# A fused attention and feed-forward kernel on one core: its list of pieces in another order

## The chip, the cores and the metric

The kernel runs on one core of one Trainium2 chip. The metric is the device time of one execution in microseconds (us), the median of the runs shown. The engines are named as in the profile: PE (TensorE, the matmuls), PEld (its weight loads), DVE (VectorE), ACT (ScalarE), POOL (GpSimd) and SP (SyncE, which issues most DMAs).

## The reference

The input x has 2048 rows of 512 numbers. The output is x plus an attention branch plus a feed-forward branch, both of the normalized x:

```python
xn = _layernorm(x, axis=-1)
return x + _A_ref(xn, A_wq, A_wk, A_wv, A_wo, A_beta) + _B_ref(xn, B_w1, B_w2)
```

The feed-forward branch is silu(xn w1) w2 with 1792 hidden columns. The attention branch has 32 heads of 16 columns and works on four segments of 512 rows. In each segment a causal softmax attention is mixed, by a gate for each head, with a linear attention that reads a memory M, z built from all segments before:

```python
for s in range(N):
    logits = jnp.einsum('bhqd,bhkd->bhqk', qs, ks) * scale + mask
    a_dot = jnp.einsum('bhqk,bhkd->bhqd', _softmax(logits), vs)
    num = jnp.einsum('bhld,bhde->bhle', phi(qs), M)
    den = jnp.einsum('bhld,bhd->bhl', phi(qs), z)[..., None] + 1e-06
    outs.append(g * num / den + (1.0 - g) * a_dot)
    M = M + jnp.einsum('bhld,bhle->bhde', phi(ks), vs)
    z = z + jnp.einsum('bhld->bhd', phi(ks))
```

Then the segments are put together and multiplied by wo.

## The kernel before

The whole kernel is cut into 1349 small pieces, and one string, ORDER, names them in the order in which their instructions are recorded. Nothing is scheduled later: each engine does its own instructions in that order, and waits on semaphores only for what its instructions need. So ORDER sets, for each engine, what stands behind what.

A word of ORDER is a piece and its numbers: the segment s first, then a tile or a part. The words that the prediction speaks of:

- `xc xd xs xq xi xg` take the sums and roots of the layer norm of a 128-row tile t, `Nv` normalizes it on DVE, `X` turns it on PE (with `Xa`, `Xv` the copies to xnT), `XD` turns it by a transposing DMA from SP instead.
- `k q v` are the products of a segment with wk, wq and wv, in parts; `kv qv vv` copy them from PSUM on DVE, `ka qa va` on ACT; `kp` and `kf` split k by odd and even heads.
- `h` is a product with w1, `ha` its tanh on ACT, `hv` the rest of the silu on DVE.
- `S0` to `S71` are the batches of scores: the matmuls into psS (line 724), the exponential from psS to a buffer Pb on ACT (line 730), and the causal selects on POOL (line 744). psS fills four PSUM banks and has one buffer, so the scores of a batch wait for the exponential of the one before.
- `E` and `O` weigh v with Pb, for even and odd heads (line 791). `Ev Ea` and `Ov` copy the sums out of PSUM and move the rows of the softmax denominators by two small DMAs each (`move_sums`); `Om` merges odd into even on DVE.
- `fp fa fv` and `gp ga gv` make phi of k and of q on POOL, ACT and DVE; `t` turns phi(k) by a transposing DMA (L441); `m` is the product for M (psM), `mv mw` add and mask it.
- `s sv r w` make the denominators and their reciprocals, `R` and `W` the same for the last segment; `z` and `d` spread them by DMAs (`spr`), `zv` and `dv` multiply, `n` is the product with M and `nv` adds it to oT.
- `o`, `oc`, `od` and `oh` are products with w2 and wo into psO, of whole, half and quarter width and of the last tile's halves. `xl` loads a tile of x again, `st` adds it and stores the output, `sh` does so for the last two halves.
- `lw` loads w2 and wo from ACT's queue, `busy` keeps PE at work while the first inputs come.

All PSUM tiles but psS share a pool of four banks, which go round in the order of ORDER: a product that takes a bank waits until the result that was there has been copied out. Products are done as one 128x128 matmul, or, between the `E`, `O` and `m` words, as four matmuls of 32 columns (`narrow`), so that the tiling of PE changes seldom.

Of the kernel before, what the change touches and what calls it, by code (L numbers as in the profile page):

```python
# [25 lines left out]
S6 fa0.3 k1.2.0 k1.2.1 k1.2.2 h0.5.0 h0.5.1 h0.5.2 q1.1.0 h0.5.3 ha0.5 k1.2.3 kv1.2 q1.1.1 q1.1.2 hv0.5
S8 h0.7.0 q1.1.3 qv1.1 h0.6.0 h0.6.1 h0.6.2 h0.6.3 ha0.6 fv0.3 E1 Ev1 k1.0.0
S9 hv0.6 h0.7.1 h0.7.2 h0.7.3 Om0 ha0.7 k1.0.1 k1.0.2 kp1.2 q1.0.0 q1.0.1 q1.0.2 fp0.1 Nv9 XD9 xs12 k1.0.3 kv1.0 kp1.0
S10 h0.8.0 hv0.7 h0.8.1 h0.8.2 h0.8.3 ha0.8 h0.9.0 h0.9.1 q1.0.3 t0.3 Nv10 XD10 h0.9.2 h0.9.3 qv1.0
S13 hv0.8 O1 Ov1 xs15 v1.0.0 v1.0.1 v1.0.2 ha0.9 v1.0.3 vv1.0 h0.10.0 h0.10.1 bmask  # L30
S12 k1.1.0 k1.1.1 k1.1.2 t0.2 k1.1.3 kv1.1 h0.10.2 h0.10.3 ha0.10 hv0.9 h1.0.0 Om1 h1.0.1 h1.0.2
# [6 lines left out]
S24 h1.8.0 h1.8.1 h1.8.2 h1.8.3 m0.0 mv0.0 q2.3.0 q2.3.1 qv2.3 ha1.8 hv1.8
S18 v2.1.0 v2.1.1 vv2.1 ga1.0 k2.0.0 o0.2.7 oc0.2.5.0 ha1.11 sv0 r0.1 o0.2.4 k2.0.1 kv2.0 xg12.4
S22 fv1.3 v2.2.0 v2.2.1 vv2.2 o0.2.1 ga1.1 gp1.2 o0.2.6 o0.0.3 o0.0.13 od0.2.11.1 hv1.11 r0.2 o0.0.10  # L40
S20 o0.2.0 oc0.0.2.0 r0.3 lw1 o0.2.2 od0.0.0.2 oc0.2.10.1 h1.1.0 h1.1.1 h1.1.2 h1.1.3 kp2.1 E4 r0.0 od0.0.0.1 ha1.1 gate w0 gv1.1 kp2.0 z0.1
S28 o0.0.6 hv1.1 z0.2 o0.0.8 z0.3 o0.0.11 o0.0.5 Ev4 oc0.0.7.1 Om3 z0.0 o0.2.8 o0.0.12 ga1.2 O4 Ov4
S26 q2.0.0 q2.0.1 h1.7.0 h1.7.1 h1.7.2 h1.7.3 gv1.2 ha1.7 qv2.0 oc0.2.10.0 od0.0.0.3 oc0.0.2.1
S23 fp1.2 od0.2.11.3 h1.4.0 hv1.7 h1.4.1 h1.4.2 Nv14 o0.2.12 h1.4.3 ha1.4 od0.2.11.0 oc0.0.7.0 zv0.3 h1.9.0 o0.2.13 h1.9.1
S25 h1.9.2 h1.9.3 ha1.9 Nv12 XD12 o0.2.3 oc0.2.5.1 gp1.0 zv0.2 o0.2.16 o0.0.16 hv1.4 zv0.0 XD14 zv0.1 E5 o0.0.17 Ev5 hv1.9
S29 fa1.2 o0.2.17 o0.2.14 k2.3.0 gv1.0 k2.3.1 kv2.3 h1.2.0 h1.2.1 h1.2.2
S27 o0.0.9 mw0.0 O5 o0.2.15 Ov5 o0.2.9 Nv13 fp1.0 XD13 h1.2.3 ha1.2 od0.2.11.2 fv1.2 st0.2 t1.2 o0.0.14 o0.0.15
S31 o0.0.4 h1.13.0 h1.13.1 h1.13.2 h1.13.3 ha1.13 o0.3.8 Om5 o0.3.11 o0.3.16 hv1.2 o0.3.9
S30 o0.3.14 h1.12.0 h1.12.1 h1.12.2 h1.12.3 t1.3 Nv15 hv1.13 ha1.12 XD15 od0.0.0.0 o0.1.16 od0.1.8.2 o0.1.17 o0.1.12 hv1.12 oc0.1.9.0
S33 o0.0.1 od0.1.8.3 o0.3.1 xl0.1 od0.1.8.0 st0.0 oc0.1.3.0 o0.1.13 oc0.1.3.1 xl0.3 gp1.3 Om4 fa1.0 o0.1.2 E6 o0.1.0  # L50
S32 kp2.3 Ev6 O6 Ov6 o0.3.17 o0.3.13 o0.3.10 o0.1.6 oc0.3.2.1 o0.1.15 m1.2 fa2.0 mv1.2 fv1.0
S35 o0.1.4 q2.2.0 q2.2.1 qv2.2 fp2.0 ga1.3 v2.0.0 v2.0.1
S34 h1.5.0 h1.5.1 o0.1.14 o0.1.11 t1.0 vv2.0 h1.5.2 oc0.3.0.1 xl1.0 gv1.3 fp1.1 h1.5.3 ha1.5 E7
# [8 lines left out]
S44 dv1.2 q3.0.0 q3.0.1 Ev9 mw1.0 oc1.2.3.1 oc1.2.11.1 od1.2.1.3 fv2.2 gp2.2 n1.2 d1.3 O8 nv1.2 fa2.3 Ov8 xl1.2 oc1.2.3.0
S45 oc1.2.11.0 o1.2.9 h2.7.0 h2.7.1 ha2.7 qv3.0 fv2.3 v3.2.0 v3.2.1 vv3.2
S48 hv2.7 h2.6.0 h2.6.1 ha2.6 k3.2.0 k3.2.1 z1.3 dv1.3 o1.0.4 dv1.0 kv3.2 ga2.2 o1.0.0 oc1.0.7.1
S47 od1.0.1.3 hv2.6 h2.0.0 od1.2.1.2 h2.0.1 ha2.0 dv1.1 zv1.3 t2.2 n1.3 Om8 o1.0.6 o1.2.5 o1.0.16 nv1.3 hv2.0 gp2.1 o1.0.13
# [877 lines left out]
```

## Time and profile before

| | us |
|---|---|
| median of the runs | 220.22 |
| lowest and highest of three | 219.97, 221.33 |
| span of the profiled execution | 218.2 |
| PE busy | 210.9 |
| PEld busy | 116.1 |
| DVE busy | 181.3 |
| ACT busy | 184.1 |
| POOL busy | 127.4 |

The span goes from the first to the last instruction of the program in the profiled execution; the profile gives no other time for that execution, and the runs' times are those of whole executions. In a row of a timeline the columns are start, duration, engine, line, operation and tiles; behind them in brackets stands the idle time before and what ended it. In a row of waits stand the engine, what it waited for, and the total, the number and the longest. In a row for a line of code the three numbers after the count are the shortest, median and longest duration in ns. In a row by stretches stand the stretch and its length, then the busy time and instruction count of PE, PEld, DVE, ACT and POOL, the granted clock, the DMA share and GB/s.

### The profile page before, as it was taken

How to read it: one execution, taken by the hardware profiler on the slowest of the kernel's cores; microseconds unless marked ns; L12 is line 12 of the kernel's file. 1: busy time of each engine (PE TensorE's matmuls, PEld its weight loads, DVE VectorE, ACT ScalarE, POOL GpSimd, SP SyncE). 2: the span in 40 equal slices, each digit the busy share in tenths (PEclk: the TensorE clock that was granted, in tenths of full speed). 3: DMA queues.
4: the chain of work that ended last, by engine and by line, in shares of the span. 5: the costliest groups of instructions: out<-in, count | busy, mean ns of one | idle time of the engine just before them, and what ended most of it. 6: DMA issues, size and time to landing. Idle time of an engine off the chain costs nothing.

```text
span 218.2 us, 9267 instructions
## 1 busy us (share of the span) xinstructions
PE 210.9 (97%) x3982; PEld 116.1 (53%) x4006; DVE 181.3 (83%) x370; ACT 184.1 (84%) x173; POOL 127.4 (58%) x203
## 2 busy tenths in 40 slices
...
ACT  3799999999999999999999999999989998942000
...
PEclk9999999999999999999999999999999999999999
...
DMA packets 33273, 19.60 MB, mean 90 GB/s; under 512 B 14672, under 2 KB 33232, under 8 KB 33232
## 3 DMA queue, kind: packets, MB, share of 16 engines
...
## 4 chain that ended last, share of the span: by engine, by line
PE 92%; DMA 3%; ACT 2%; issue 1%; SPq 1%; DVE 0%
PE ps L336 26%; PE psO L338 17%; PE ps L338 16%; PE psS L724 11%; PE psO L336 9%; PE psV L791 8%; PE psS L338 4%; DMA wk_sb<-in_A_wk_dram 3%; ACT Pb L730 2%; PE psM L452 1%; SPq L169 0%; SPq L158 0%; PE ps L509 0%; ACT th L492 0%; DVE o_half L668 0%
## 5 line engine op out<-in xcount | busy, mean ns | idle before, releaser
L730 ACT ACTIVATE Pb<-psS 128x2048 bf16<-128x2048 f32 x72 | 135.2, 1878 | 4.7 <-PE psS L724 2.4
L744 POOL TENSOR_SCALAR_AFFINE_SELECT Pb<-Pb 128x512 bf16<-128x512 bf16 (+2 forms) x88 | 62.3, 718 | 22.4 <-ACT Pb L730 19.6
L497 DVE SCALAR_TENSOR_TENSOR hT<-th,ps 128x512 bf16<-128x512 bf16 x56 | 38.0, 682 | 10.1 <-ACT th L492 9.4
L744 POOL TENSOR_SCALAR_AFFINE_SELECT lows<-Pb 64x512 bf16<-64x512 bf16 (+1 forms) x40 | 24.3, 607 | 32.0 <-ACT Pb L730 24.9
L338 PE MATMUL psO<-w_sb,hT 128*32 128x512 bf16 (+2 forms) x696 | 41.4, 321 | 0.0
L336 PE MATMUL ps<-xnT,w_sb 128*128 128x512 bf16 (+1 forms) x177 | 35.9, 330 | 0.2 <-issue 0.2
L492 ACT ACTIVATE th<-ps 128x512 bf16<-128x512 f32 x56 | 33.0, 594 | 3.5 <-PE ps L338 3.1
L338 PEld LDWEIGHTS <-hT 128*32 128x32 bf16 x864 | 21.5, 96 | 14.6 <-issue 3.1
L338 PE MATMUL ps<-xnT,w_sb 128*32 128x512 bf16 (+1 forms) x408 | 24.8, 349 | 0.0
L724 PE MATMUL psS<-qT,k 32*128 32x64 bf16 (+3 forms) x512 | 23.0, 233 | 0.2
L336 PEld LDWEIGHTS <-w_sb 128*128 128x128 bf16 x178 | 16.4, 98 | 11.9 <-issue 1.2
L336 PE MATMUL psO<-w_sb,hT 128*128 128x512 bf16 (+2 forms) x82 | 20.5, 324 | 0.7 <-issue 0.6
L791 PEld LDWEIGHTS <-Vz 128*32 128x32 bf16 x768 | 16.1, 97 | 9.5 <-issue 0.6
L791 PE MATMUL psV<-Pb,Vz 128*32 128x448 bf16 (+7 forms) x512 | 21.0, 286 | 0.0
L724 PEld LDWEIGHTS <-k 32*128 32x128 bf16 x512 | 9.3, 92 | 21.2 <-issue 20.4
L336 PE MATMUL ps<-xnT,wk_sb 128*128 128x256 bf16 (+1 forms) x63 | 14.4, 326 | 0.4 <-DMA wk_sb<-in_A_wk_dram 0.2
L724 PE MATMUL psS<-qT,kT 16*128 16x448 bf16 (+3 forms) x256 | 14.7, 269 | 0.0
L338 PEld LDWEIGHTS <-w_sb 128*32 128x32 bf16 x408 | 10.3, 96 | 6.7 <-issue 1.7
L621 DVE SCALAR_TENSOR_TENSOR o_out<-psO,x_res 128x512 bf16<-128x512 f32 x14 | 9.4, 679 | 5.0 <-PE psO L338 3.9
L336 PEld LDWEIGHTS <-hT 128*128 128x128 bf16 x92 | 8.5, 98 | 9.6 <-issue 2.1
L828 DVE CAST odd<-psV 128x512 bf16<-128x512 f32 x16 | 11.0, 687 | 2.4 <-PE psV L791 2.4
L338 PE MATMUL psO<-wo_sb,oT 128*32 128x512 bf16 x140 | 12.8, 379 | 0.0
...
## 6 DMA issues: line engine op xcount, KB each, us to landing
...
```

The source lines that it names most:

```text
L336: return [nc.tensor.matmul(out, lhsT=lhsT, rhs=rhs, start=start, stop=stop, skip_group_check=True)]
L338: nc.tensor.matmul(out[c : c + 32], lhsT=lhsT[:, c : c + 32], rhs=rhs, start=start, stop=stop, tile_position=(0, c), skip_group_check=True,)
L452: nc.tensor.matmul(psM[32 * g : 32 * g + 32, i, :].rearrange("p (r d) -> p r d", d=DH), lhsT=st["phiK", dt][:, j, 32 * g : 32 * g + 32], r ...
L492: nc.scalar.activation(out=th[:], in_=sts[s]["h", ft][:, :], func=AF.Tanh, scale=0.5)
L497: nc.vector.scalar_tensor_tensor(out=st["hT"][:, ft, :], in0=st.pop(("th", ft))[:], scalar=1.0, in1=st.pop(("h", ft))[:, :], op0=ALU.add, ...
L621: out = nc.vector.scalar_tensor_tensor(out=o_out[:], in0=st.pop(("psO", j)), scalar=0.5, in1=st["x", j][:], op0=ALU.mult, op1=ALU.add)
L724: nc.tensor.matmul(psS[:, g, c : c + q2 - q1], lhsT=keys[rows], rhs=st["qT"][rows, dt, q1:q2], start=True, stop=True, tile_position=(32 * ...
L730: exp = nc.scalar.activation(out=blocks(Pb, b).rearrange("p y g c -> p g y c"), in_=psS[:, :, :].rearrange("p g (y c) -> p g y c", c=BLOCK ...
L744: over[id(Pb)].append(nc.gpsimd.affine_select(out=out, in_=in_, compare_op=ALU.is_ge, fill=0.0, base=base, pattern=[[0, out.shape[1]], [1, ...
L791: nc.tensor.matmul(psV[32 * g : 32 * g + 32, q0 : q0 + nq].rearrange("p (y c) -> p y c", y=weights.shape[2]), lhsT=Vzs[s % 2][:, kt, 4 * d ...
L828: copy(out=odd[:], in_=sts[s].pop(("psV", 1))[:, :])
```

## The change

ORDER is the same 1349 words in another order. No function, buffer, load or instruction's form changes, but some products pass between the one wide and the four narrow matmuls, since that follows from the words around them: PE has 4003 matmuls in place of 4006. The sequence of the batches `S` is the same. The diff, cut to lines that the prediction speaks of:

```diff
-S3 h0.3.0 h0.3.1 q0.3.1 q0.3.2 h0.3.2 tanh XD5 h0.3.3 k0.3.0 Nv7 XD7 q0.3.3 qv0.3 k0.3.1 xs8 ha0.3
-S4 Nv4 h0.1.0 k0.3.2 h0.1.1 hv0.3 XD4 h0.2.0 h0.2.1 h0.2.2 h0.2.3 ha0.2 xs9 k0.3.3 kv0.3 hv0.2
...
-S17 h1.10.3 k1.3.0 hv1.0 k1.3.1 k1.3.2 k1.3.3 kv1.3 fp1.3 h0.12.0 h0.12.1 xs14 m0.2 mv0.2 ha1.10 h0.12.2
-S21 fv0.1 q1.3.0 q1.3.1 q1.3.2 q1.3.3 qv1.3 h1.3.0 hv1.10 gp1.1 h0.12.3 ha0.12 t0.1 h1.3.1 h1.3.2 t0.0 h1.3.3
-S14 hv0.12 k2.2.0 h0.11.0 h0.11.1 k2.2.1 h0.11.2 h0.11.3 xl0.0 h0.13.0 ha1.3
...
-S42 kv3.0 o1.2.6 o1.2.2 o1.2.10 d1.1 h2.11.0 h2.11.1 ha2.11 o1.2.0 t2.0 vv3.0 zv1.1 gv2.3 o1.2.4 fp2.2 zv1.2
-S39 hv2.11 q3.2.0 ga2.1 q3.2.1 qv3.2 d1.0 v3.3.0 v3.3.1 va3.3 E9
...
+S3 q0.3.1 hv0.0 h0.3.0 h0.3.1 fp0.0 h0.3.2 q0.3.2 q0.3.3 k0.3.0 h0.3.3 Nv5 qv0.3 ha0.3
+S4 k0.3.1 h0.1.0 h0.2.0 h0.1.1 XD6 XD5 XD4 tanh h0.2.1 Nv7 h0.2.2 hv0.3 h0.2.3 ha0.2 h0.1.2 k0.3.2 fp0.2
...
+S17 h1.10.3 Ov2 hv1.0 k1.3.0 k1.3.1 k1.3.2 k1.3.3 h0.12.0 ha1.10 m0.2 h0.12.1 kv1.3
+S21 h0.12.2 h0.12.3 Om0 q1.3.0 kp1.1 q1.3.1 q1.3.2 mv0.2 h1.3.0 hv1.10 bmask fv0.1 q1.3.3 ha0.12 h1.3.1 h1.3.2
+S14 h0.11.0 qv1.3 h0.11.1 k2.2.0 k2.2.1 h1.3.3 xs14 h0.11.2 hv0.12 gp1.1 mw0.2 ha1.3 h0.11.3 t0.0
...
+S42 o1.2.2 o1.2.0 o1.2.6 gv2.3 h2.11.0 od1.2.1.1 vv3.0 ga2.1 z1.1 fv2.2 h2.11.1 ha2.11 zv1.2 xl1.2 o1.2.10 dv1.2 o1.2.4 kv3.0
+S39 q3.2.0 v3.3.0 v3.3.1 va3.3 z1.3 od1.2.1.3 hv2.11 fp2.3 q3.2.1 E9
...
```

At the start the words from the turn of x tile 2 on are `X2.1 Xa1.1 k0.1.0 tb Nv3 X3.1 Xv2.1 k0.1.1` before and `X2.1 xi3 Nv3 Xa1.1 tb X3.1 Xv2.1 k0.0.0` now. In the last line, of S71, the stretch that the prediction adds up reads now:

```
od2.3.10.3 o3.2.0 o3.2.15 o3.0.16 oh13.1 od3.1.0.0 n3.0 o3.2.10 o3.1.4 od3.0.3.1 oc3.1.10.1 st2.3 Om15 xl3.0 o3.1.16 o3.0.10 oh9.0 nv3.0 zv3.3 oh14.1
```

Two places show how the instructions move. The first is SP's queue between the copies of the sums of O0 and the product m0.2. The rows into zraw are the small moves of `move_sums`, those into xnT transposes of x tiles (`XD`), those into phiK the two turns of phi(k) that m0.2 needs (`t0.3` and `t0.2`), and x_res is `xl0.2`. Before:

```order
L813 DMA zraw_102<-odd_740 4x256 x2
L813 DMA zraw_102<-oraw_869 4x256 x2
L857 DMA_TRANSPOSE xnT_139<-xn_t_911 128x4x128
L441 DMA_TRANSPOSE phiK_960<-pk_850 128x4x128
L857 DMA_TRANSPOSE xnT_139<-xn_t_962 128x4x128
L813 DMA zraw_102<-odd_1024 4x256 x2
L441 DMA_TRANSPOSE phiK_1085<-pk_635 128x4x128
L614 DMA x_res_1139<-in_A_x_dram 128x512
L857 DMA_TRANSPOSE xnT_139<-xn_t_1147 128x4x128
```

And now, from the same moves of O0 on:

```order
L813 DMA zraw_102<-odd_759 4x256 x2
L441 DMA_TRANSPOSE phiK_786<-pk_642 128x4x128
L813 DMA zraw_102<-oraw_884 4x256 x2
L857 DMA_TRANSPOSE xnT_139<-xn_t_926 128x4x128
L614 DMA x_res_1044<-in_A_x_dram 128x512
L813 DMA zraw_102<-odd_1050 4x256 x2
L857 DMA_TRANSPOSE xnT_139<-xn_t_946 128x4x128
L441 DMA_TRANSPOSE phiK_1090<-pk_844 128x4x128
L857 DMA_TRANSPOSE xnT_139<-xn_t_944 128x4x128
```

One turn of phi(k) (t0.2) has moved ahead of the transposes of x; the other (t0.3) has moved behind the load x_res, the next moves of odd sums and a second transpose of x. The load x_res takes the buffer that the transpose just ahead of it reads.

The second place is DVE's queue in the last 15 us of the program. The rows L608 are `nv3.1`, `nv3.0` and `nv3.3`, L589 are `zv`, L835 is `Om15`, and the first L621 is `st2.3`. Before:

```order
L608 TENSOR_TENSOR oT_5227<-ps_5283,oT_5227 128x512
L589 TENSOR_TENSOR oT_5227<-spr_5202,oraw_4205 128x512
L835 COPY_PREDICATED oraw_5018<-omask_130,odd_5022 128x256
L608 TENSOR_TENSOR oT_5227<-ps_5344,oT_5227 128x512
L589 TENSOR_TENSOR oT_5227<-spr_5307,oraw_5018 128x512
L608 TENSOR_TENSOR oT_5227<-ps_5403,oT_5227 128x512
L621 SCALAR_TENSOR_TENSOR o_out_5451<-psO_4858,x_res_5354 128x512
```

And now:

```order
L608 TENSOR_TENSOR oT_5318<-ps_5348,oT_5318 128x512
L621 SCALAR_TENSOR_TENSOR o_out_5435<-psO_4846,x_res_5190 128x512
L835 COPY_PREDICATED oraw_5001<-omask_130,odd_5020 128x256
L608 TENSOR_TENSOR oT_5318<-ps_5414,oT_5318 128x512
L589 TENSOR_TENSOR oT_5318<-spr_5363,oraw_5001 128x512
L608 TENSOR_TENSOR oT_5318<-ps_5459,oT_5318 128x512
```

The store of the last tile of segment 2 has moved from behind the last two additions to oT to a place ahead of both.

More of the change, by code (lines that the diff above doesn't have):

```diff
@@ L26 @@
[L26 to L31, printed above, removed]
@@ L38 @@
[L38 to L42, printed above, removed]
@@ L43 @@
[L43 to L53, printed above, removed]
@@ L60 @@
-S42 kv3.0 o1.2.6 o1.2.2 o1.2.10 d1.1 h2.11.0 h2.11.1 ha2.11 o1.2.0 t2.0 vv3.0 zv1.1 gv2.3 o1.2.4 fp2.2 zv1.2
-S39 hv2.11 q3.2.0 ga2.1 q3.2.1 qv3.2 d1.0 v3.3.0 v3.3.1 va3.3 E9
[L62 to L65, printed above, removed]
@@ new lines @@
+S13 hv0.8 kp1.0 ha0.9 h0.10.0 h0.10.1 xs15 O1 XD8 v1.0.0 xl0.2 v1.0.1 Ov1 XD11 v1.0.2 v1.0.3
+S12 h0.10.2 vv1.0 h0.10.3 h1.0.0 hv0.9 xs13 h1.0.1 k1.1.0 t0.3 k1.1.1 XD10 k1.1.2 h1.0.2 ha0.10 XD9 k1.1.3 kv1.1
+S15 hv0.10 h1.0.3 E2 ha1.0 h1.10.0 h1.10.1 Om1 Ev2 h1.10.2 O2
+S17 h1.10.3 Ov2 hv1.0 k1.3.0 k1.3.1 k1.3.2 k1.3.3 h0.12.0 ha1.10 m0.2 h0.12.1 kv1.3
+S21 h0.12.2 h0.12.3 Om0 q1.3.0 kp1.1 q1.3.1 q1.3.2 mv0.2 h1.3.0 hv1.10 bmask fv0.1 q1.3.3 ha0.12 h1.3.1 h1.3.2
+S14 h0.11.0 qv1.3 h0.11.1 k2.2.0 k2.2.1 h1.3.3 xs14 h0.11.2 hv0.12 gp1.1 mw0.2 ha1.3 h0.11.3 t0.0
```

103 lines of the change are left out of this document (63 added, 40 removed).

## The prediction

> **What bounds the kernel now.** First the page: busy shares, slices, and the chain that ended last.
>
> ```profile
> span 218.2 us, 9267 instructions
> PE 210.9 (97%) x3982; PEld 116.1 (53%) x4006; DVE 181.3 (83%) x370; ACT 184.1 (84%) x173; POOL 127.4 (58%) x203
> ACT  3799999999999999999999999999989998942000
> PEclk9999999999999999999999999999999999999999
> PE 92%; DMA 3%; ACT 2%; issue 1%; SPq 1%; DVE 0%
> ```
>
> TensorE is busy in 97% of the span at full clock and holds 92% of the chain. ScalarE is as full until about 190 us and then has nothing to do. Busy time can hide small waits, since one matmul's record overlaps the next, so I read the busy time by stretches, then PE's own waits.
>
> ```profile
> 12.00:190.00 178.00, 175.54 (x3263) 92.32 (x3286) 154.89 (x311) 172.78 (x153) 121.86 (x185) 1.00 0.32 80
> 0.00:12.00 12.00, 10.09 (x102) 8.37 (x105) 8.75 (x26) 6.87 (x16) 4.24 (x16) 1.00 0.84 274
> PE psS L864 <- DVE zraw L188: 1.1, 1, 1.1
> PE psO L336 <- issue: 1.0, 6, 0.2
> PE ptr L845 <- DVE xn_t L315: 0.5, 1, 0.5
> PE ps L336 <- DMA wk_sb<-in_A_wk_dram: 0.2, 1, 0.2
> ```
>
> From 12 to 190 us PE is idle for 178.00 - 175.54 = 2.46 us, and its list of waits names no engine there that costs more than 0.2 us. The named waits lie in the first 9 us. So the next question is what one round, from one batch of scores (line 724) to the next, is made of. The timeline of PE and of ACT over two rounds:
>
> ```profile
> 104.88 0.21 PE L724 MATMUL psS<-qT,k 32*128 32x64 bf16 x4
> 107.26 0.21 PE L724 MATMUL psS<-qT,k 32*128 32x64 bf16 x4
> 107.60 1.90 PE L336 MATMUL ps<-xnT,w_sb 128*128 128x512 bf16 x8
> 109.34 0.38 PE L336 MATMUL psO<-w_sb,hT 128*128 128x512 bf16 x1
> 109.65 0.40 PE L724 MATMUL psS<-qT,k 32*128 32x64 bf16 x8
> 105.33 1.88 ACT L730 ACTIVATE Pb<-psS 128x2048 bf16<-128x2048 f32 x1
> 107.10 0.58 ACT L376 CAST kT<-ps 128x512 bf16<-128x512 f32 x1
> 107.72 1.88 ACT L730 ACTIVATE Pb<-psS 128x2048 bf16<-128x2048 f32 x1
> 109.49 0.59 ACT L492 ACTIVATE th<-ps 128x512 bf16<-128x512 f32 x1
> ```
>
> A round takes 107.26 - 104.88 = 2.38 us. Eight products take 109.34 - 107.60 = 1.74 us, 0.217 each. Two loops close at the same length: PE's (the scores and nine products) and that of scores and exponential, for psS has one buffer: the exponential that starts at 105.33 ends at 107.21, the next scores start at 107.26. A round with one small ScalarE instruction beside the exponential cannot be shorter than 2.38. First and last batch:
>
> ```profile
> L724 PE MATMUL psS<-qT,k x512: 184/198/348, 12.0 to 190.1; 32*128 32x64 bf16 x104, 32*128 32x192 bf16 x24, 32*128 32x448 bf16 x22, 32*128 32x320 bf16 x21
> ```
>
> 71 rounds take 178.1 us. By columns, the matmuls between them are 740.75 products of 512: 740.75 x 0.217 = 160.7, which leaves 17.4 / 71 = 0.245 us a round for entering and leaving the row-tiled scores. There is hardly anything in this stretch to be won by order; there is something to be lost.
>
> **The change part by part.** It removes no work. Both lists have the same 1349 words, the batches of scores in the same sequence, and 144 changes of PE's tiling. Some products pass from the four narrow matmuls to one wide one or back, for no time:
>
> ```profile
> 107.67 1.83 PE ps L336 x8
> 117.36 1.84 PE ps L338 x32
> ```
>
> Eight wide matmuls take 1.83, 32 narrow ones 1.84. Up to the last batch the new list has 741.25 products, half a product more, and half a product fewer behind it: zero.
>
> *The start.* The transposes of x tile 3 (X3) now stand ahead of the first product of k.
>
> ```profile
> 6.59 0.40 PE L845 MATMUL ptr<-ident,xn_t 128*128 128x128 bf16 x4 [0.52 <-DVE xn_t L315]
> 8.54 0.39 PE L336 MATMUL ps<-xnT,wk_sb 128*128 128x256 bf16 x2 [0.24 <-DMA wk_sb<-in_A_wk_dram]
> 8.77 0.39 PE L845 MATMUL ptr<-ident,xn_t 128*128 128x128 bf16 x4
> PEld L724 <- ACT qT L399: 0.3, 1, 0.3
> ```
>
> X3 can fill the 0.24 us in which PE waits for wk. But the first scores wait for ScalarE's copy of q in any case, and that comes behind the same two copies. Between 0 and -0.24; taken: 0, since the wait for qT (0.3) swallows it.
>
> *Short rounds.* Only a round with less than 2.38 us of PE work costs anything. S3 has one product less and S4 one more than before, which is an exchange. S17 loses a quarter of h0.12 to the next round; before, S17's round is
>
> ```profile
> 48.55 0.40 PE L724 MATMUL psS<-qT,k 32*128 32x192 bf16 x8
> 50.98 0.40 PE L724 MATMUL psS<-qT,k 32*128 32x192 bf16 x8
> ```
>
> 50.98 - 48.55 = 2.43; less 0.217 is 2.21, so PE waits 2.38 - 2.21 = 0.17 us for the exponential. Term: +0.17. Behind it the queue of PE alone waits.
>
> *Rounds with two small ScalarE instructions.* One such instruction moves from S18 to S22, from S39 to S42, from S48 to S47 and from S56 to S50. A round with two needs on ACT 1.77 + 0.6 + 0.6 = 2.97 (starts 105.33, 107.10, 107.72), and together with the next round 2.97 + 2.38 = 5.35 between the first scores and the last. PE's work over the two, at 0.217 a product and 0.245 a round: S22 with S20 22.75 products, 5.43; S42 with S39, S47 with S46 and S50 with S52 22 products each, 5.26. The old S39 with S44 had 21.75, 5.21, and PE's list of waits has none there. Between 0 and 0.09 for each of three; taken: 0.05 in all.
>
> *VectorE, whose results give PE's banks back.* psS takes four PSUM banks, the other four go round; a late copy stops PE. In the new list many VectorE words stand nearer to the PE word that needs them (33 of 170 edges within 0.25 us of PE's work, before 12 of 171). But the engine runs when its inputs are there, not at its place in the list. Adding up its queue with the rows' durations ahead of each such edge, 33 of PE's waits (those of the scores left out) had under 0.25 us to spare before and 36 have it now: no net loss, but new thin places, at O15 (behind the store st2.1), k2.2.0, k2.1.0 and q2.1.0. Before, such margins cost nothing. Bounds: 0, and at O15 a whole store; taken 0.2.
>
> *The end.* VectorE's store st2.3 now stands ahead of nv3.0. Rows of before:
>
> ```profile
> 206.79 0.69 DVE L608 TENSOR_TENSOR oT<-ps,oT 128x512 bf16<-128x512 f32 x1 [0.72 <-PE ps L338]
> 205.62 0.45 DVE L835 COPY_PREDICATED oraw<-omask,odd 128x256 int32<-128x256 int32 x1
> 209.46 0.69 DVE L621 SCALAR_TENSOR_TENSOR o_out<-psO,x_res 128x512 bf16<-128x512 f32 x1 [0.45 <-PE psO L338]
> 215.31 0.42 DVE L668 SCALAR_TENSOR_TENSOR o_half<-psS,x_res 128x256 bf16<-128x256 f32 x1 [0.18 <-PE psS L338]
> ```
>
> From od2.3.10.3 to oh14.1, which needs nv3.0, PE has 10 products, 2.17 us; VectorE needs 0.16 (a matmul's 0.38 less its 0.217) + 0.69 + 0.45 + 0.69 = 1.99. It fits. The last instructions stay PE's last half-product, the 0.42 us o_half and its store. Term: 0.
>
> Sum: 218.2 + 0.17 + 0.05 + 0.2 = 218.6 us of span. The three runs of before have a median of 220.22, 2.0 over the profiled span (219.97 to 221.33): 220.6.
>
> **The rivals.** *Slower by VectorE behind GpSimd.* What VectorE does on SBUF alone is uneven, what reads PSUM is not:
>
> ```profile
> L835 DVE COPY_PREDICATED oraw<-omask,odd x16: 384/468/1143, 37.7 to 205.6; 128x256 int32<-128x256 int32 x16
> L589 DVE TENSOR_TENSOR oT<-spr,oraw x16: 408/422/839, 77.6 to 207.4; 128x512 bf16<-128x512 bf16 x16
> L497 DVE SCALAR_TENSOR_TENSOR hT<-th,ps x56: 672/680/690, 20.2 to 199.4; 128x512 bf16<-128x512 bf16 x56
> ```
>
> A stretched copy takes 1.143 - 0.384 = 0.76 us more. If one falls just ahead of each of three thin edges (a predicated copy, Om13, does stand ahead of st2.1 and O15), PE loses 3 x 0.7 = 2.1: 222.7. Against it: the medians (0.468 and 0.422) lie near the minimum, so most such copies are not held up, and of the thin edges of before none was hit. It decides from three hits on. The Trainium skill, "SBUF — State Buffer", section Who interferes with whom, says that VectorE and GpSimd share a port pair as an exclusive lock: the one that starts second waits out the other's whole instruction. These rows agree (uneven on SBUF alone, even from PSUM). By that rule a hit costs up to one GpSimd select; with the median of the row below, three cost 2.0, and the sum would be 222.6 in place of 222.7.
>
> ```profile
> L744 POOL TENSOR_SCALAR_AFFINE_SELECT Pb<-Pb x88: 409/657/1096, 14.9 to 192.7; 128x512 bf16<-128x512 bf16 x32, 128x256 bf16<-128x256 bf16 x32, 128x1024 bf16<-128x1024 bf16 x24
> ```
>
> *Slower by a late transposing DMA.* SP's order changes: t0.3, the last turn of pk that m0.2 needs, now comes behind xl0.2, which waits until XD8 has landed, Ov1's two moves and XD11. Adding up SP's queue, it is issued some 3.6 us ahead of m0.2; with a landing of 2.4 (an estimate, twice the issue of the row below) 1.2 us are left, before over 3. The upper bound is the one landing that the chain shows:
>
> ```profile
> L441 SPq DMA_TRANSPOSE phiK<-pk x12: 1191/1216/1275, 39.7 to 139.7; - x12
> 2.68 5.81 DMA wk_sb<-in_A_wk_dram
> ```
>
> At 5.81 PE would stand 5.81 - 2.4 - 1.2 = 2.2 us: 222.8. Against it: the engines are lightly used there, unlike at 2.68.
>
> *Faster.* If the new order took away all 2.46 us that PE idles between 12 and 190, it would be 217.8. Nothing in the list does, as every round is held by two loops.
>
> **How the numbers follow.** No change to speak of, 220.6, own range 219.7 to 222.0: 0.78. GpSimd rival 0.11, late DMA 0.07, faster 0.02, other stalls of over 2 us 0.02. A measurement of this kernel tells about 1% (2.2 us) from no change; so faster 0.02, within 1% 0.78, slower 0.20. The range goes from 219.5 (no stall, the start's 0.24 won, the lowest run's 1.8 beside the span: 219.7, and 0.2 for the runs' own spread) to 223.0, past both rivals.
>
> **What would show it.** Right: PE busy near 175.5 between 12 and 190, first and last scores again near 12.0 and 190.3, no PE wait for DVE or DMA over 0.3 us, S17 to S21 at 2.38, nv3.0 done before oh14.1. Wrong: a later last batch of scores with waits of PE for DVE at O15, k2.2.0, k2.1.0 or q2.1.0, or at psM for phiK; or a first batch well before 11.9.

## The result

The changed kernel takes 222.97 us, the median of six runs (221.47 to 224.20); the kernel before took 220.38 beside it (219.87 to 221.33). The ratio is 1.0122, with a 95% interval of 1.0088 to 1.0155: slower by 2.6 us where no change was forecast. Here and below the ratios leave out two runs of the kernel before, of 736.97 us (beside e0 to e3) and 223.50 us (beside e4 to e7), which lie over 1.5% above its fastest. The list of waits of the changed kernel's TensorE (what waited, for what, total, times, longest) and its chain by engine:

```profile
span 221.5 us, 9262 instructions
PE 64%; ACT 9%; DVE 8%; DMA 6%; POOL 5%; issue 3%; SPq 2%; DVEq 0%; POOLq 0%; ACTq 0%
PE psS L864 <- DVE zraw L188: 1.1, 1, 1.1
PE ps L338 <- DVE hT L497: 1.0, 1, 1.0
PE ptr L845 <- DVE xn_t L315: 0.8, 1, 0.8
PE psV L791 <- POOL Pb L744: 0.8, 1, 0.8
```

The span is 3.2 us longer than before's (3.3 by the rounded figures). The chain says that it is no longer one engine's: PE had 92% of it and has 64%, the rest lies with ACT, DVE, DMA and POOL. The second and fourth rows of the waits are new; the first and third lie ahead of the first scores.

Where the time went can be read without any guess, since both lists have the same 72 batches of scores in the same order. The first matmul of line 724 of each batch, from the timelines of PE, gives this difference to before in us (left: its start in the kernel before; the other columns are the experiments below). Each column is one execution; that of e2 and of e3 is the slowest run of its kernel, that of e9 the fastest. So the columns say where time is lost, and the medians say how much.

```
batch before  after     e0     e1     e2     e3     e5     e6     e8    e11     e7     e9    e10
S0     11.95  +0.15  +0.27  +0.22  +0.32  -0.05  +0.13  +0.40  +0.59  +0.23  +0.18  -0.22  +0.12
S4     21.55  +0.11  +0.24  +0.19  +0.28  +0.75  +0.10  +0.36  +0.56  +0.20  +0.17  -0.23  +0.11
S7     23.93  +0.15  +0.28  +0.22  +0.32  +1.34  +0.13  +0.40  +0.59  +0.23  +0.18  -0.22  +0.12
S17    48.55  +0.58  +0.71  +0.63  +1.04  +1.93  +0.65  +0.82  +1.07  +0.84  +0.18  -0.20  +0.15
S21    50.98  +0.53  +0.66  +0.58  +0.99  +1.87  +0.60  +0.76  +1.01  +0.79  +0.18  -0.20  +0.14
S28    71.21  +0.53  +0.66  +0.59  +0.99  +1.87  +0.60  +0.77  +1.02  +0.79  +0.18  -0.20  +0.15
S26    73.62  +0.64  +0.77  +0.70  +1.10  +1.99  +0.71  +0.88  +1.13  +0.90  +1.07  -0.20  +0.15
S25    78.45  +0.63  +0.76  +0.69  +1.10  +1.98  +0.70  +0.87  +1.13  +0.89  +1.06  -0.20  +0.14
S29    80.84  +1.58  +1.73  +0.69  +2.07  +1.98  +0.70  +0.87  +1.13  +0.89  +1.16  -0.20  +0.14
S61   147.29  +1.68  +1.83  +0.79  +2.17  +2.08  +0.80  +0.97  +1.22  +0.99  +1.18  -0.03  +0.17
S54   150.00  +1.35  +2.38  +0.46  +2.62  +2.65  +1.51  +0.65  +0.90  +0.66  +1.17  -0.03  +1.04
S62   167.03  +1.31  +2.34  +0.42  +2.58  +2.62  +1.47  +0.61  +0.85  +0.62  +1.17  -0.03  +0.95
S63   169.59  +2.83  +3.86  +1.94  +2.79  +2.83  +1.69  +0.82  +1.07  +0.84  +1.17  +2.22  +0.94
S67   171.99  +2.89  +3.92  +2.00  +3.29  +3.33  +1.75  +0.88  +1.13  +0.89  +1.17  +2.22  +0.95
S65   179.34  +2.93  +3.96  +2.04  +3.33  +3.37  +1.79  +0.92  +1.17  +0.94  +1.76  +2.21  +0.94
S66   181.89  +3.10  +4.13  +2.21  +4.46  +3.97  +3.62  +1.34  +1.34  +1.11  +1.76  +2.22  +0.95
S71   189.99  +2.99  +4.02  +2.10  +4.35  +3.86  +3.51  +1.23  +1.23  +1.00  +1.76  +2.21  +0.94
end   218.24  +3.22  +4.13  +2.04  +4.30  +3.79  +3.46  +1.18  +1.17  +0.95  +1.77  +2.23  +0.97
```

In the column "after" two steps carry the loss: S25 to S29 (0.95) and S62 to S63 (1.52). A step also holds the work that was moved from one round to another, 0.217 us for each product. Counting the matmuls between the batches in both traces takes this out: S61 to S54 (-0.33) has one and a half products fewer and loses nothing, and S62 to S63 has one product more and loses 1.30. Rounds with the same work that take longer are S8 to S9 (0.15) and S15 to S17 (0.25); S17 to S21 has one product less and gains only 0.05, so it loses 0.17. With the start (0.15) that makes 2.97 in all; the table has 2.99 at S71.

**S25 to S29.** The timeline of POOL from the select of S22 to that of S23 (start, duration, tiles, in brackets the idle time before and what ended it), in the kernel before, with the products of E5 on PE that read the last of them, and then in the changed one:

```profile
67.11 0.51 POOL L297 TENSOR_SCALAR rstd_all<-mv_all 128x4 f32<-128x4 f32 x1
67.70 1.02 POOL L300 TENSOR_TENSOR rstd_all<-rstd_all,expo 128x4 f32<-128x4 f32 x1
68.79 0.66 POOL L744 TENSOR_SCALAR_AFFINE_SELECT lows<-Pb 64x512 bf16<-64x512 bf16 x1
79.26 0.63 POOL L744 TENSOR_SCALAR_AFFINE_SELECT Pb<-Pb 128x512 bf16<-128x512 bf16 x1
79.97 0.72 PE L791 MATMUL psV<-Pb,Vz 128*32 128x512 bf16 x16
```

```profile
68.83 0.65 POOL L744 TENSOR_SCALAR_AFFINE_SELECT lows<-Pb 64x512 bf16<-64x512 bf16 x1 [1.28 <-ACT Pb L730]
69.55 1.09 POOL L744 TENSOR_SCALAR_AFFINE_SELECT Pb<-Pb 128x1024 bf16<-128x1024 bf16 x1
70.73 0.71 POOL L297 TENSOR_SCALAR rstd_all<-mv_all 128x4 f32<-128x4 f32 x1
71.53 1.02 POOL L300 TENSOR_TENSOR rstd_all<-rstd_all,expo 128x4 f32<-128x4 f32 x1
76.96 0.86 POOL L385 TENSOR_SCALAR k<-kT,pm_odd 128x512 bf16<-128x512 bf16 x1
77.79 0.71 POOL L385 TENSOR_SCALAR k<-kT,pm_even 128x256 bf16<-128x256 bf16 x1
80.53 1.76 POOL L744 TENSOR_SCALAR_AFFINE_SELECT Pb<-Pb 128x512 bf16<-128x512 bf16 x2
81.55 0.72 PE L791 MATMUL psV<-Pb,Vz 128*32 128x512 bf16 x14 [0.77 <-POOL Pb L744]
```

L297 and L300 are the word `xg12.4`, the roots for x tiles 12 to 15. Before, they filled POOL's idle time ahead of S22's select. Now POOL idles there for 1.28 us, and the two instructions (0.71 and 1.02) stand behind that select; from there on the queue has hardly a gap until S23's select (the first of the two at 80.53), for which E5 waits 0.77 us. Before, this select ended at 79.26 + 0.63 = 79.89, and E5's products that read it started at 79.97: an edge with 0.08 us to spare.

**S62 to S63.** SP's issues of the spreads in the changed kernel (two for each), and from its chain the transfer:

```profile
159.30 4.17 SPq L577 DMA_DIRECT2D spr<-rz  x6
164.02 1.27 SPq L577 DMA_DIRECT2D spr<-rz  x2
```

```profile
164.69 3.89 DMA spr<-rz
168.60 0.03 DVE phiQT L599
```

Then DVE's timeline and PE's:

```profile
166.68 0.42 DVE L599 TENSOR_TENSOR phiQT<-spr,phiQT 128x512 bf16<-128x512 bf16 x1
168.60 0.63 DVE L599 TENSOR_TENSOR phiQT<-spr,phiQT 128x512 bf16<-128x512 bf16 x1 [1.50 <-DMA spr<-rz]
169.15 1.30 DVE L589 TENSOR_TENSOR oT<-spr,oraw 128x512 bf16<-128x512 bf16 x1
170.38 1.27 DVE L497 SCALAR_TENSOR_TENSOR hT<-th,ps 128x512 bf16<-128x512 bf16 x2
171.11 0.40 PE L338 MATMUL ps<-phiQT,Mbf 128*32 128x512 bf16 x4 [0.95 <-DVE hT L497]
```

The first six are `d2.2`, `z2.0` and `d2.0`, the last two `d2.3`, which lands 3.9 us after the issue of its second half began. `dv2.3` (168.60) stops DVE for 1.50 us, `zv2.0` behind it takes 1.30 instead of 0.42, and only then come `hv3.1` and `hv3.12`. The first of these empties the bank that `n2.0` needs, and PE stands for 0.95. `dv2.3` is itself stretched, 0.63 for 0.42.

### The profile page after: what moved, and what is told of

Read it like the earlier page. It is cut to its first block, busy times and chain, and to the rows that moved or that the text cites. A ratio compares the mean times of both kernels' runs of the same rounds, so it can differ in the third digit from the quotient of the medians.

```text
span 221.5 us, 9262 instructions
## 1 busy us (share of the span) xinstructions
PE 212.2 (96%) x3979; PEld 115.5 (52%) x4003; DVE 180.9 (82%) x370; ACT 184.2 (83%) x173; POOL 126.3 (57%) x203
## 4 chain that ended last, share of the span: by engine, by line
PE 64%; ACT 9%; DVE 8%; DMA 6%; POOL 5%; issue 3%; SPq 2%; DVEq 0%; POOLq 0%; ACTq 0%
PE ps L336 18%; PE ps L338 11%; PE psO L338 10%; PE psS L724 8%; PE psO L336 7%; PE psV L791 7%; ACT Pb L730 7%; DMA spr<-rz 5%; POOL Pb L744 3%; SPq L577 2%; POOL k L385 1%; PE psS L338 1%; DMA x_lo<-in_A_x_dram 1%; DVE stats L286 1%; POOL lows L744 1%
## 5 line engine op out<-in xcount | busy, mean ns | idle before, releaser
L744 POOL TENSOR_SCALAR_AFFINE_SELECT lows<-Pb 64x512 bf16<-64x512 bf16 (+1 forms) x40 | 23.1, 578 | 36.8 <-ACT Pb L730 35.2
L338 PE MATMUL psO<-w_sb,hT 128*32 128x512 bf16 (+2 forms) x700 | 42.0, 322 | 0.0
L336 PE MATMUL ps<-xnT,w_sb 128*128 128x256 bf16 (+1 forms) x178 | 38.6, 328 | 0.5 <-issue 0.2
L338 PE MATMUL ps<-xnT,w_sb 128*32 128x512 bf16 (+1 forms) x376 | 24.2, 353 | 0.0
L336 PEld LDWEIGHTS <-w_sb 128*128 128x128 bf16 x186 | 17.0, 98 | 13.6 <-issue 2.5
L336 PE MATMUL psO<-w_sb,hT 128*128 128x512 bf16 (+2 forms) x85 | 21.6, 325 | 0.1
L385 POOL TENSOR_SCALAR k<-kT,pm_odd 128x512 bf16<-128x512 bf16 x15 | 10.6, 706 | 9.4 <-ACT kT L376 8.4
L336 PE MATMUL ps<-xnT,wk_sb 128*128 128x512 bf16 (+1 forms) x62 | 14.2, 328 | 0.3 <-issue 0.2
L338 PEld LDWEIGHTS <-w_sb 128*32 128x32 bf16 x376 | 9.2, 96 | 7.0 <-issue 1.9
```

The lines of the kernel that those rows point to most:

```text
L336: return [nc.tensor.matmul(out, lhsT=lhsT, rhs=rhs, start=start, stop=stop, skip_group_check=True)]
L338: nc.tensor.matmul(out[c : c + 32], lhsT=lhsT[:, c : c + 32], rhs=rhs, start=start, stop=stop, tile_position=(0, c), skip_group_check=True,)
L385: nc.gpsimd.tensor_scalar(out=to, in0=frm, scalar1=keep[:, 0:1], scalar2=1.0, op0=ALU.mult, op1=ALU.mult)
L744: over[id(Pb)].append(nc.gpsimd.affine_select(out=out, in_=in_, compare_op=ALU.is_ge, fill=0.0, base=base, pattern=[[0, out.shape[1]], [1, ...
```

## The experiments

The queue theory: the loss is made of words that stand in a queue (POOL's, SP's, DVE's) behind something that is late, and one of them is a transfer; each such place can be removed or made by moving one word. The port theory: the loss is in stretched instructions, DVE's and POOL's held up by each other. The two do not exclude each other: an instruction that is late can meet another that stretches it. In the diffs one word stands on a line with its neighbours.

**e0_after** is the changed kernel again, beside e1 to e3.

> The changed kernel again, beside the others of this call. Both theories: 222.0 to 223.5 us, 1.0 to 1.5% over before, and the same two waits of TensorE in its profile: about 0.8 us for GpSimd's select at E5 (S25 to S29 over 3.1 us) and about 1.0 us for VectorE's hT ahead of n2.0 (S62 to S63 over 3.8 us).

Measured: 223.54 (222.57 to 224.37), ratio 1.0125 (1.0093 to 1.0157). Both waits are there (S25 to S29 +0.97, S62 to S63 +1.52), and a third that the first profile did not have. SP's rows and PE's for phiK:

```profile
141.26 3.34 SPq L441 DMA_TRANSPOSE phiK<-pk  x2
147.34 1.21 SPq L441 DMA_TRANSPOSE phiK<-pk  x1
151.84 0.28 PE L452 MATMUL psM<-Vz,phiK 128*32 128x32 bf16 x16 [0.74 <-DMA phiK<-pk]
```

The first two turns took 3.34 us to issue where they took 2.54 in the first profile, so `t2.1` came 0.6 later, and m2.0 waited for it. From its issue to its use lie 151.84 - 147.34 = 4.5 us.

**e1_root**: `xg12.4` ahead of S22.

```diff
 k2.0.1
+xg12.4
 S22
...
 o0.2.0
-xg12.4
 hv1.11
```

> The changed kernel with one word put back: xg12.4, the two GpSimd instructions (0.71 and 1.02 us) that form rstd of x tiles 12 to 15, stand ahead of the selects of S22 again, where GpSimd waits for ScalarE. Queue theory: all of GpSimd's work up to the select of S23 comes 0.8 us sooner, E5's wait of 0.77 goes, S25 to S29 falls from 3.34 to about 2.5, and the time by 0.8 us (to about 0.3% under the changed kernel). Port theory (the stretched instructions of GpSimd beside VectorE, 0.86 and 0.71 where 0.69 and 0.48 are usual, make the wait): the stretch stays, E5 still waits 0.4 us or more, and the time falls by less than 0.4 us.

Measured: 221.93 (221.19 to 222.64), ratio 1.0067 (1.0046 to 1.0087). S25 to S29 lost nothing any more (+0.00). POOL:

```profile
71.74 0.66 POOL L744 TENSOR_SCALAR_AFFINE_SELECT Pb<-Pb 128x512 bf16<-128x512 bf16 x1 [0.86 <-ACT Pb L730]
76.23 0.70 POOL L385 TENSOR_SCALAR k<-kT,pm_odd 128x512 bf16<-128x512 bf16 x1
76.90 0.68 POOL L385 TENSOR_SCALAR k<-kT,pm_even 128x256 bf16<-128x256 bf16 x1
79.92 0.64 POOL L744 TENSOR_SCALAR_AFFINE_SELECT Pb<-Pb 128x512 bf16<-128x512 bf16 x1
```

POOL has idle time again (0.86 ahead of S20's select), and S23's select ends at 80.56 for a product that starts at 80.67, without a wait. The second half of `kp2.1` is still long (0.68), and it does not matter. The queue theory holds here. The median fell by 1.6 us, more than the 0.95 of the step and twice the forecast: e0's profile has the wait for phiK, e1's has not, and how often the other runs had it is not known.

**e2_mul** and **e3_both**: `dv2.3` and `zv2.0` behind `hv3.12`; e3 with e1's edit too.

```diff
 h3.1.1
-dv2.3
 h3.12.1
...
 od2.0.6.1
-zv2.0
 od2.0.6.0
...
 hv3.12
+dv2.3
+zv2.0
 o2.0.9
```

> The changed kernel with two VectorE words, dv2.3 and zv2.0, put behind hv3.1 and hv3.12, so that VectorE does not stand still for the spread of d2.3 (landed at 168.57) while hv3.1, which n2.0's bank waits for, is ready behind it. Queue theory: n2.0's wait of 0.95 goes, S62 to S63 falls from 4.08 to about 2.8, the time by 1.0 to 1.3 us. Rival (late transfer: what is late is the spread itself, and everything that needs it is only moved): nv2.0 or a later product waits in its place, and the time falls by less than 0.4 us. Port theory: zv2.0 stays stretched at 1.3 us, but now only nv2.0 stands behind it; also little left, 0.3 us or less.

> The changed kernel with both edits: xg12.4 ahead of S22's selects, dv2.3 and zv2.0 behind hv3.12. Queue theory: both waits gone, the two gains add up, 1.8 to 2.1 us less than the changed kernel: about 220.9 to 221.2, within 0.5% of before; left over are the start (0.14), S9 to S10 (0.17), S12 to S24 (0.2), S28 to S25 (0.1), the end (0.3). If the waits are one slack that only moves from place to place: less than 1.2 us, 1.0% over before stays at 0.5% or more.

Measured: e2 222.89 (222.05 to 224.27), ratio 1.0106 (1.0074 to 1.0138), 0.65 us under e0 where 1.0 to 1.3 was forecast; e3 223.07 (221.75 to 223.76), ratio 1.0108 (1.0080 to 1.0137). The wait at n2.0 went in both (S62 to S63 +0.21), but it came back: 0.50 at S63 to S67 in place of 0.06, since `nv2.0`, Ev13 and what stands behind them on DVE were now late, and 1.13 (e2) or 0.60 (e3) at S65 to S66 in place of 0.17, in both behind another late spread, for which DVE waits 1.67 and 1.15. So the rival was half right: with `zv2.0` moved as well, part of the wait only moves on. e3 missed its forecast by 2 us. Its profile has no E5 wait, but a wait for phiK (S61 to S54 +0.57) and one near the start that no other profile has. DVE's timeline and PE's there:

```profile
19.07 0.70 DVE L286 BATCH_NORM_STATS2 stats<-x_hi 128x6 f32<-128x512 bf16 x1 [0.73 <-DMA x_hi<-in_A_x_dram]
19.90 1.21 DVE L315 TENSOR_SCALAR xn_t<-x_hi,mv_all,rstd_all 128x512 bf16<-128x512 bf16 x1
21.77 0.38 PE L336 MATMUL ps<-xnT,wk_sb 128*128 128x256 bf16 x2 [0.86 <-DVE Vz L406]
```

`xs9` stopped DVE until the x tiles 8 to 11 had landed, with the copy `vv0.3` behind it. The words there are those of the changed kernel; in its own profile the tiles were there in time (18.46). So the new list waits for transfers at three places (the x tiles, phiK, `d2.3`), and the first two hit in some runs and not in others.

**e4_root_t**: e1 with `t2.1` ahead of two stores and a load in SP's queue.

```diff
 Ov10
+t2.1
 st1.0
...
 E11
-t2.1
 Ev11
```

> The changed kernel with xg12.4 ahead of S22's selects and, besides, the transposing DMA t2.1 ahead of the stores st1.0 and st1.2 and the load xl3.1 in SP's queue (issued some 1.8 us sooner). In three of five profiles of this list so far TensorE waited 0.7 to 0.8 us for phiK at m2.0 (S61 to S54); in the two others it did not. Late-transfer theory: t2.1, issued 4.1 us ahead of m2.0, lands with nothing to spare, and the move takes the wait away in every run: no wait for phiK in the profile, median about 0.3 us under that of xg12.4 alone (221.9), highest run under 222.2. Rival (the wait comes from the DMA engines, not from the place in the queue): phiK is still waited for in some runs, median 221.7 to 222.2, runs as far apart as before (1.5 us).

Measured: 221.55 (220.65 to 223.79), ratio 1.0058 (1.0029 to 1.0088). No wait for phiK in the profile, and the median is 0.4 under e1's, close to the forecast 0.3; but one profile says little, and the runs lie further apart than e1's, up to 223.79 where under 222.2 was forecast: by itself inconclusive. (Its column, left out of the table, has S25 to S29 at 0.00 and S62 to S63 at 1.53.) Of the profiles of the changed list without this edit, four have the wait (e0, e2, e3, e5) and two do not (the first, e1): in the four the two turns ahead of `t2.1` took 3.3 to 3.5 us to issue, in the two 2.54; of those with it (e4, e6, e8, e11) none has, and e10 makes it in the other list.

**e5_root_d** and **e6_three**: e1 with `d2.2` put behind `ha3.8`, and e1 with `d2.2` and `t2.1` moved.

```diff
 gp3.1
-d2.2
 o1.3.11
...
 ha3.8
+d2.2
 S64
```

> The changed kernel with xg12.4 ahead of S22's selects and the spread d2.2 issued behind ha3.8, where the list before has it, not ahead of z2.0, d2.0 and d2.3. Queue theory: d2.3 is issued 1.3 us sooner and no longer lands behind six other halves, dv2.3 starts without a wait, n2.0's wait of 0.95 goes, and unlike with VectorE's words moved nothing is given back at S63 to S67 (+0.44) and S65 to S66 (+0.4 to +1.0): 1.2 us under xg12.4 alone, 220.5 to 220.9, within 0.3% of before. Rival (VectorE has 1.5 us more work there, mw2.0 ahead of S59 and zv2.0 at 1.30 for 0.42, and would be late without the spread too): less than 0.5 us.

> All three: xg12.4 sooner, t2.1 sooner, d2.2 later. If the three waits are independent: the profile names no wait of TensorE over 0.4 us behind the first scores, last scores 0.6 to 1.0 us later than before (start 0.2, S9 to S10 0.17, S12 to S24 0.2, S28 to S25 0.1), time 220.6 to 221.2, 0.1 to 0.4% over before. If a fourth wait takes their place: 0.7% or more over before.

Measured: e5 222.33 (221.68 to 223.97), ratio 1.0088 (1.0057 to 1.0120); e6 221.40 (220.62 to 223.46), ratio 1.0043 (1.0015 to 1.0071). In both S62 to S63 fell from +1.52 to +0.22 with DVE's order as in the changed kernel. So DVE's load of work there was not the cause; without the late spread nothing is lost. In e6 `dv2.3` still waited 0.55 for it, from 166.41 to 166.96, and that cost PE nothing. e6 lies just over its forecast of 220.6 to 221.2. e5 missed its time: phiK was late (+0.71 at S54), and S65 to S66 took 1.83 longer than before, in place of 0.17 (0.41 in e6). DVE's row there in e5:

```profile
181.66 0.83 DVE L589 TENSOR_TENSOR oT<-spr,oraw 128x512 bf16<-128x512 bf16 x1 [1.98 <-DMA spr<-rz]
```

`d2.2` now stood ahead of `z2.1` in SP's queue, and `zv2.1` waited for that: the edit had moved the late transfer, not removed it.

**e8_three_z**: e6 with `z2.1` ahead of `d2.2`, as in the list before.

```diff
 ha3.8
+z2.1
 d2.2
 S64
...
 o2.0.17
-z2.1
 o2.0.2
```

> The changed kernel with xg12.4 and t2.1 sooner, d2.2 behind ha3.8, and z2.1 now ahead of d2.2 (as the list before has the two). With d2.2 ahead of it, z2.1 was issued 1.3 us later and VectorE stood still for it ahead of zv2.1, which cost 0.25 us (three words) to 1.7 us (two words) at S65 to S66. Late-transfer theory: that goes, S65 to S66 is back at +0.16; 220.6 to 221.2, 0.1 to 0.35% over before, last scores 0.6 to 1.0 us later than before. Rival (VectorE's and GpSimd's stretched instructions move on to the next place): 0.5% or more over before, with a wait of TensorE for VectorE over 0.4 us at another word.

Measured: 220.70 (220.43 to 221.47), ratio 1.0011 (0.9995 to 1.0027). Four moved words of 1349 take the changed list back to the time of the kernel before, and its runs lie within 1.0 us in place of 2.7. S65 to S66 is at +0.17, and the profile names no wait over 0.2 us behind the first scores. Its last scores come 1.23 later than before, of which 0.59 is already there at the first scores in this run.

**e11_root_t_dv**: e4 with `dv2.3` alone behind `hv3.12`.

```diff
 h3.1.1
-dv2.3
 h3.12.1
...
 hv3.12
+dv2.3
 o2.0.9
```

> The changed kernel with xg12.4 and t2.1 sooner and dv2.3 alone put behind hv3.12; zv2.0 stays ahead of hv3.1, d2.2 stays early. Late-transfer theory: only the wait for d2.3 stopped VectorE, zv2.0 (its spread landed long before) runs at once; n2.0's wait of 0.95 goes and nothing is given back at S63 to S67, where moving zv2.0 too had cost 0.44: 1.2 us under xg12.4 and t2.1 alone (221.55), 220.3 to 220.8. Port theory (zv2.0's 1.30 us beside GpSimd's select is what n2.0 waits for): n2.0 still waits 0.4 us or more, 221.0 or more.

Measured: 220.89 (220.53 to 223.54), ratio 1.0028 (1.0002 to 1.0053). S62 to S63 +0.22, which is the one product more, S63 to S67 +0.05: nothing is given back. The median lies between the forecasts (220.3 to 220.8, and 221.0 or more for the port theory), so the trace has to decide. DVE:

```profile
166.00 0.42 DVE L599 TENSOR_TENSOR phiQT<-spr,phiQT 128x512 bf16<-128x512 bf16 x1
166.33 0.42 DVE L589 TENSOR_TENSOR oT<-spr,oraw 128x512 bf16<-128x512 bf16 x1
168.01 1.28 DVE L497 SCALAR_TENSOR_TENSOR hT<-th,ps 128x512 bf16<-128x512 bf16 x2 [1.26 <-ACT th L492]
```

Without the wait for `d2.3`, `zv2.0` runs at 0.42, and DVE even has 1.26 us to spare ahead of `hv3.1`. No wait comes in its place. But the edit took away both the wait and the stretch, so it does not tell how the two share the loss.

**The reverse.** Three runs put one place of the changed list into the kernel before: e7 `xg12.4` behind S22's select, e9 `dv2.3` and `zv2.0` ahead of `hv3.1`, e10 `t2.1` behind the stores.

```diff
 kv2.0
-xg12.4
 S22
+xg12.4
 fv1.3
```

> The reverse: the kernel before with xg12.4 alone moved behind S22's selects, as the changed kernel has it, all else unchanged. Queue theory: GpSimd loses the idle time ahead of S22's selects, its queue up to S23's selects ends about 1.0 us later, and E5, which in the profile of before starts its second half 0.08 us after the select it needs, waits 0.8 to 1.0: time 1.0225 x 0 + 0.8 to 1.0 us over before (0.35 to 0.45%), S25 to S29 at 3.2 or more. Port theory, or a wait that needs more than this word: under 0.3 us.

(Its "1.0225 x 0 +" is a slip of the pen; the forecast is 0.8 to 1.0 us.) Measured: 221.21 (220.66 to 221.94), ratio 1.0024 (1.0007 to 1.0041): 0.6 us, clear of noise but under the forecast. The profile has the wait, of about the forecast size but three rounds sooner:

```profile
72.56 0.61 POOL L417 TENSOR_SCALAR pos<-qT 128x512 bf16<-128x512 bf16 x1
73.14 0.83 POOL L744 TENSOR_SCALAR_AFFINE_SELECT Pb<-Pb 128x512 bf16<-128x512 bf16 x1
74.02 0.62 PE L791 MATMUL psV<-Pb,Vz 128*32 128x448 bf16 x16 [0.70 <-POOL Pb L744]
```

In the list before `gp1.2` (72.56) stands ahead of S20's select, so O4 is hit first (S28 to S26 +0.89), and E5 only 0.10 more. This column also has +0.59 at S64 to S68, where PE waits 0.41 for DVE's addition `nv2.3`; that lies far behind the moved word and is not put down to it.

```diff
 ha3.1
+dv2.3
+zv2.0
 hv3.1
...
 n2.0
-zv2.0
 nv2.0
...
 o2.0.10
-dv2.3
 h3.4.0
```

> The reverse for n2.0: the kernel before with dv2.3 and zv2.0 put ahead of hv3.1, as the changed kernel has them, d2.3 issued where it was. Late-transfer theory: VectorE stands still for d2.3 (issued until 167.17, at least 1.6 us to land) with hv3.1 behind it, n2.0 waits for hv3.1 instead of starting at 168.90: S62 to S63 1.0 to 2.0 us longer than 2.55, time 0.4 to 0.9% over before. Port theory (only the stretch of zv2.0 costs): at most 0.4 us.

Measured: 223.02 (222.19 to 224.85), ratio 1.0125 (1.0082 to 1.0168): above the forecast of 0.4 to 0.9%. But its three slowest runs (223.35 to 224.85) had a granted clock of 0.992; the three at 1.000 (222.19, 222.33, 222.69) have a median 0.8% over before, inside the forecast. The profile is one of these. The issue of the spread's two halves by SP, then DVE's rows and PE's:

```profile
165.81 1.33 SPq L577 DMA_DIRECT2D spr<-rz  x2
168.72 0.43 DVE L599 TENSOR_TENSOR phiQT<-spr,phiQT 128x512 bf16<-128x512 bf16 x1 [1.62 <-DMA spr<-rz]
169.07 0.83 DVE L589 TENSOR_TENSOR oT<-spr,oraw 128x512 bf16<-128x512 bf16 x1
169.82 1.27 DVE L497 SCALAR_TENSOR_TENSOR hT<-th,ps 128x512 bf16<-128x512 bf16 x2
170.55 0.40 PE L338 MATMUL ps<-phiQT,Mbf 128*32 128x512 bf16 x4 [1.68 <-DVE hT L497]
```

The same wait, made by two words: 1.68 here and 0.20 behind it, S62 to S63 +2.25. The stretch of `zv2.0` is 0.83 - 0.42 = 0.41 of this, so the port theory's bound of 0.4 is passed by far: here the transfer is the larger part.

```diff
 fv2.1
-t2.1
 gp2.0
...
 E11
+t2.1
 Ev11
```

> The reverse for phiK: the kernel before with t2.1 alone put behind st1.2, st1.0 and xl1.1 in SP's queue (issued at about 145.6 instead of 139.73), 3.5 us ahead of m2.0 at 149.05. Late-transfer theory, with the 4.3 us from issue to use that the changed kernel's profiles with a wait show: TensorE waits 0.3 to 0.9 us for phiK between S61 and S54, time 0.2 to 0.4% over before. Rival (the long landing belongs to t2.2 and t2.3 issued one right behind the other, which is not so here): a landing near 2.4, no wait, same time as before within 0.1%.

Measured: 221.05 (220.26 to 222.88), ratio 1.0031 (1.0006 to 1.0056). SP and PE:

```profile
145.80 1.21 SPq L441 DMA_TRANSPOSE phiK<-pk  x1
150.23 0.28 PE L452 MATMUL psM<-Vz,phiK 128*32 128x32 bf16 x16 [0.74 <-DMA phiK<-pk]
```

4.4 us again from the issue to the use, with no other transposing DMA right ahead of it: the rival falls. The runs lie 2.6 us apart.

Put together, as the part of 1.0125 that each edit gives back: `xg12.4` 0.58%, `t2.1` 0.09% more, then `dv2.3` 0.30% more, or `d2.2` with `z2.1` 0.47% more, which leaves 0.11% (-0.05 to 0.27). For `xg12.4` and for `d2.2` with `z2.1` the intervals before and after the edit lie apart; for `t2.1` and for `dv2.3` alone they overlap, and there the traces carry the argument. What lies between 0.11% and nothing is not told apart.

## Why the prediction was wrong

The time lies at the top of the range (to 223.0), but it is slower by over 1%, where the forecast was no change. That it lies inside, and close to what the two slower rivals gave (222.7 and 222.8), is luck: neither the three hits at thin places nor the late t0.3 took place. Two steps failed: the sum of VectorE's queue, which left out waits for transfers, and GpSimd's queue, which had no term at all. By its steps:

- *What bounds the kernel*: right. The rounds that wait for nothing go on at before's length, and from S29 to S61 the difference moves by 0.10 us in 66, which is the half product more.
- *Zero for the products that change their tiling*: nothing in the table speaks against it. Of the 39 rounds whose work changed, 34 moved by 0.217 us a product to within 0.03. The others are S17 and S62, named above, the exchange of S3 and S4, and S57, with half a product more for no time.
- *The start*, 0: it cost 0.15, and between -0.22 and 0.59 in the other profiles of both lists.
- *Short round S17*, +0.17: right. S17 to S21 takes 51.51 - 49.13 = 2.38, as forecast, with one product less than in the 2.43 of before:

```profile
49.13 0.40 PE L724 MATMUL psS<-qT,k 32*128 32x192 bf16 x8
51.51 0.40 PE L724 MATMUL psS<-qT,k 32*128 32x192 bf16 x8
```

- *Rounds with two small ScalarE instructions*, +0.05: around the rounds named the difference moves by 0.00 (S18 to S28), 0.05 (S38 to S46) and 0.05 (S53 to S52), and the last two have a quarter of a product more, which is 0.05. So they cost nothing, the lower bound. S8 to S9, not among them, lost 0.15, since two small ScalarE instructions came later ahead of S8's exponential (its start moved from 34.49 to 34.93).
- *VectorE*, +0.2: this step failed. The sum of its queue against PE's counted durations only. It found 36 edges under 0.25 us in place of 33 and called that no net loss; O15, k2.2.0, k2.1.0 and q2.1.0, the thin places that it named, were not hit. What it left out is that a word in the queue can itself wait: `dv2.3` stands directly behind `dv2.0` in the new list, and DVE reached it at 167.10, 3.1 us after the transfer's issue began (164.02). Measured, this place cost 1.3 us.
- *GpSimd's queue*: this step failed too. It was not added up at all, although the selects are what E and O wait for. At S25 to S29 it cost 0.95. At S15 to S17 it seems to be behind the 0.25: O2 waits 0.09 for a select (47.67) that stands behind a split of k (46.57 to 47.71), and then runs slower than before. No run tried that place.
- *The late DMA rival*, 0.07: right in kind, wrong in place and size. t0.3 did no harm; t2.1 did, in some runs. The landing, taken as 2.4 from twice the issue, was 4.4 to 4.5 us from the issue to the use in e0 and e10, which waited for it. By that figure the sum would have found t2.1: in the first profile of the changed list it is issued at 146.74 and m2.0 starts at 150.67, 3.9 us, where it had 9.3 before (139.73 to 149.05). That profile names no wait there, so the landing varies from run to run.
- *The port rival*, 0.11: not as it was put. No three hits at thin places; but stretched instructions do stand in the chain. In the changed kernel `zv2.0` starts at 169.15 beside POOL's select:

```profile
169.03 1.16 POOL L744 TENSOR_SCALAR_AFFINE_SELECT Pb<-Pb 128x1024 bf16<-128x1024 bf16 x1
```

It ends at 170.45, 0.26 behind the select's end at 170.19. But for 0.16 (its own 0.42 less 0.26) this agrees with the rule of the Trainium skill, "SBUF — State Buffer", section Who interferes with whom, that the second of the two waits out the other's instruction. In this profile DVE lost 1.50 to the transfer, 0.21 to the stretch of `dv2.3` and 0.88 to that of `zv2.0`, together 2.59, of which about 1.6 was slack (2.59 - 0.95). So by this sum neither the transfer (1.50) nor the stretches (1.09) alone would have cost PE anything. e1, with the same words at this place, bears it out. Its rows of DVE and POOL:

```profile
167.43 0.91 DVE L599 TENSOR_TENSOR phiQT<-spr,phiQT 128x512 bf16<-128x512 bf16 x1 [1.22 <-DMA spr<-rz]
168.26 1.30 DVE L589 TENSOR_TENSOR oT<-spr,oraw 128x512 bf16<-128x512 bf16 x1
167.41 0.66 POOL L744 TENSOR_SCALAR_AFFINE_SELECT lows<-Pb 64x512 bf16<-64x512 bf16 x1 [1.50 <-ACT Pb L730]
```

The transfer was 0.28 less late, but `dv2.3` now met a select itself (0.91 for 0.42), `zv2.0` took 1.30 as before, and DVE lost 1.22 + 0.49 + 0.88 = 2.59 and PE 0.96 again. In e6 both words started before this select (at 166.96 and 167.30, the select at 167.60), ran at 0.43 and 0.42, and PE lost nothing. So in the changed list the late transfer counts because it pushes the two words into POOL's selects. No run took away the selects alone.
- *The end*, 0: right. From S71 to the last instruction the first profile takes 0.23 us longer, e0 0.11, and the other profiles of the changed list 0.05 to 0.07 less than before.
- *What would show it*: PE's busy time was the wrong sign to watch. From 12 to 190 it fell to 173.90 because PE waited, and with the stretch taken to the last scores it reads:

```profile
12.00:193.00 181.00, 176.90 (x3265) 92.00 (x3289) 153.60 (x309) 172.97 (x154) 121.53 (x186) 1.00 0.32 77
```

PE idles 4.1 us in it, where it idled 2.46 in the stretch of before: of the 3.0 us that the stretch is longer, 1.6 are idle and 1.4 are counted as busy, so the starts of the scores show the loss and the busy time does not.
